# Bucketed attention and two dense layers on one core: preparing head pairs earlier and taking the products with v later

## The chip, the cores and the metric

The kernel runs on one core of a Trainium2 chip. Five engines matter here: TensorE (PE, with its weight loads PEld), VectorE (DVE), ScalarE (ACT), GpSimd (POOL) and SyncE (SP), which only issues transfers to the 16 DMA engines. The metric is device time in microseconds (us) for one execution; the lower the better.

## The reference

Two batches of eight heads, 768 positions, 64 numbers each. Queries and keys are hashed with six random projections; a query sees only the keys in its own bucket.

```
q_bits = (q @ proj > 0);  k_bits = (k @ proj > 0)        # six bits each
mask   = bucket(q_bits)[:, None] == bucket(k_bits)[None, :]
scores = where(mask, q @ k.T / sqrt(D), -1e9)
attn   = exp(scores - max(scores));  attn /= sum(attn) + 1e-9
x      = attn @ v                                        # (B, H, S, D) -> (B*S, 512)
h = x @ w_in1;  x = (h * sigmoid(1.702 * h)) @ w_out1    # 512 -> 2048 -> 512
h = x @ w_in2;  x = (h * sigmoid(h)) @ w_out2
```

The weights arrive as 64-bit floats and are turned into pairs of 32-bit tiles (high part, low part) on the chip.

## The kernel before

The attention is cut into 96 steps: 16 heads of six query chunks of 128 rows. Heads go in pairs, twelve steps to a pair, and the first 48 steps are the first batch. A step passes through these functions:

- `scores(j)`: four matmuls on PE into two PSUM banks (L417, L418); the second of each two adds the mask through the rows of bits in BQ and BK.
- `top(j)`: DVE takes the row minimum and writes the tile p (L425). `exps(j)`: ACT takes the exponential in place (L430).
- `p_high(j)`: ACT or DVE rounds p to 16 bits into one half of a tile hl (L439, L441). `p_low(j)`: POOL writes the rest into the other half (L445). One hl tile holds two steps.
- `p_turn(j)`: on every second step SP issues one DMA transpose of 128 x 3072 16-bit numbers, hl to pt (L451).
- `av(j)`: 18 pairs of weight load and matmul on PE, in three kinds (L463 to L465), multiply pt with the scaled v in VS.
- `norm(g)`: after the last step of a group DVE divides, PE turns the result (L491), ACT and DVE split it into XH and XL (L497, L498), the inputs of the dense layers.

Before a pair's steps, its preparation `ahead(pr, s)` is spread over steps s from -4 to 7: `natural` rounds and splits q and k as loaded, `turn` and `evict` transpose them through PE and ACT, `move` brings them into BQ (a transfer on SP) and BK (a copy on ACT) in the first batch, `bits` and `signs` make the hash bits, and `rows` issues four transfers on SP that put them into BQ and BK. `v_max`, `v_spread`, `v_scale` find the scale of v; `v_high` (ACT, L396) and `v_low` (DVE, L405) write the scaled v into VS. There are two VS tiles, so a pair writes over the one of two pairs before.

The loop emits the work of position i in an order written out by hand: scores of step i + 2, products with v of step i - LAG, and so on. A planner then sorts each engine's instructions by this order, moved up by the offsets in SOONER, and by its own picture of the time. Each engine runs its list in order. SP's list holds the transposes, the loads, the moves, the rows, the fetched weights (L139) and the spilled ones (L186).

From the end of the first batch's loop (SWITCH) the tiles of the pool att2 are given back, and the first layer on the first batch (`mlp`, L632 for the first product, L666 for the second, L637 for the first gate activation) is interleaved with the second batch's attention. After that the rest of both layers runs alone. MORE gives how many extra tiles of a kind the pool att2 holds during the first batch.

Of the kernel before, what the change touches and what calls it, by code (L numbers as in the profile page):

```python
# [10 lines left out]
F32R = mybir.dt.float32r  # L11
# [10 lines left out]
def tile_lsh_attention_two_mlps(  # L22
# [13 lines left out]
    V, A, G, T, SP = nc.vector, nc.scalar, nc.gpsimd, nc.tensor, nc.sync  # L36

    B, H, S, D = q.shape
    NB = proj.shape[1]
    NT, DM = out.shape  # L40
    DFF = w_in1.shape[1]
    P = 128
    NC = S // P
    HS = S // 2
    HC = NC // 2
    HEADS = B * H
    NPAIR = H // 2
    NDC = DM // P
# [3 lines left out]
    TB = HS  # L52
# [7 lines left out]
    QSCALE = -1.0 / math.sqrt(D)  # L60
    assert math.frexp(QSCALE)[0] == -0.5
    NBUF = 3
    LAG = 3
    TUL = 1
    MORE = {'aq': 1, 'ak': 1, 'p': 1, 'hl': 1, 'pt': 0, 'nk': 1, 'nq': 1, 'nv': 1}
    PTB = 2
    EARLY = 0
    WSTART = 38
# [10 lines left out]

    SOONER = ({'ahead': 100, 'move': 20, 'load_v': 400, 'evict': 200, 'p_high': 200, 'natural': 800, 'p_turn': 35, 'turn': 100, 'p_low': 75, 'top': 35, 'exps': 75, 'bits': 300, 'norm': 35, 'load': 50, 'signs': 20}, {'scores': 200, 'evict': 50, 'norm': 300, 'av': 400, 'natural': 200, 'gate': 50, 'p_turn': 20, 'load_v': 200, 'load': 20, 'sum': 150, 'move': 20, 'p_high': 150, 'rows': 100, 'p_low': 75, 'bits': 100, 'exps': 20}, {'gate': 300, 'sum': 10, 'weights': 50})  # L80
    RATE = (3.4, 2.85)
    SWITCH = HEADS // 2 * NC + LAG + 1
    RING = 3
    RING2 = 6

# [6 lines left out]
    xpool = ctx.enter_context(tc.tile_pool(name="x", bufs=1))  # L92
    wpool = ctx.enter_context(tc.tile_pool(name="w", bufs=RING))
    spill = ctx.enter_context(tc.tile_pool(name="spill", bufs=1, space=bass.MemoryType.DRAM))

    XH = [xpool.tile([P, NDC, TB], F32R, name=f"XH{i}") for i in range(NT // TB)]
    XL = [xpool.tile([P, NDC, TB], F32R, name=f"XL{i}") for i in range(NT // TB)]

# [151 lines left out]
    def attention(sp, s1, ps_m, ps_v, ahead_of, setup):  # L252
        nat, st = {}, {}
# [12 lines left out]
        N = len(steps)  # L266
# [141 lines left out]
        def scores(j):  # L408
            n, c = steps[j]
            aq, ak = st["q", n], st["k", n]  # L410
            bq, bk = BQ[place(n)], BK[place(n)]
            ps = ahead_of["pool"].tile([P, 2, 512], F32, tag="s", name="pss")
            lq = aq.rearrange("p a b -> p (a b)")[:, c * P:(c + 1) * P]
            bq = bq[:, c * P:(c + 1) * P]
            for half in range(2):
                o = ps[:, half, 0:HS]
                T.matmul(o, lhsT=lq, rhs=ak[:, half, :], start=True, stop=False)  # L417
                T.matmul(o, lhsT=bq, rhs=bk[:, half * HS:(half + 1) * HS], start=False, stop=True)  # L418
            st["S", j] = ps[:, :, 0:HS]


# [32 lines left out]
        def av(j):  # L454
            (n, c), g = steps[j], group[j]
            vs, s = st["v", n // 2]
            pt = st.pop(("pt", j))
            if j == g[0]:
                st["av", g] = v_bank("pav")
            o = st["av", g][:, c * (D + 1):(c + 1) * (D + 1)]  # L460
            for i in range(NC):
                hv, lv = vs[:, n % 2, i, 0:D + 1], vs[:, n % 2, i, D + 1:]
                T.matmul(o, lhsT=pt[:, i], rhs=hv, start=(i == 0), stop=False)  # L463
                T.matmul(o[:, 0:D], lhsT=pt[:, i], rhs=lv, start=False, stop=False)  # L464
                T.matmul(o, lhsT=pt[:, NC + i], rhs=hv, start=False, stop=(i == NC - 1))  # L465


        def norm(g):
# [32 lines left out]
        asked = set()  # L501
# [6 lines left out]
        def ahead(pr, s):  # L508
            a, b = 2 * pr, 2 * pr + 1

            two = bool(ahead_of["more"]) and b + 2 < HEADS // 2 + 2
            loads = {
                1: [(load, a + 2, "k"), (load, b + 2, "k")],
                3: [(load, a + 2, "q"), (load, b + 2, "q")],
                4: [(load_v, pr + 1)],
            } if two else {
                -3: [(load, b, "k")],
                -1: [(load, b, "q")],
                1: [(load, a + 2, "k")],
                3: [(load, a + 2, "q")],  # L520
                8: [(load_v, pr + 1)],
            }
            return [(f, *x) for f, *x in {
                -4: [(natural, a, "k")],
                -3: [(turn, a, "k", 0)],
                -2: [(evict, a, "k", 0), (turn, a, "k", 1), (natural, a, "q")],
                -1: [(evict, a, "k", 1), (turn, a, "q", 0), (v_max, pr)],
                0: [(evict, a, "q", 0), (turn, a, "q", 1), (natural, b, "k"), (move, a, "k")],
                1: [(evict, a, "q", 1), (turn, b, "k", 0)],
                2: [(turn, b, "k", 1), (v_spread, pr), (natural, b, "q"), (move, a, "q")],  # L530
                3: [(evict, b, "k", 0), (evict, b, "k", 1), (turn, b, "q", 0), (v_scale, pr)],
                4: [(evict, b, "q", 0), (turn, b, "q", 1), (v_high, pr, 0), (move, b, "k")],
                5: [(evict, b, "q", 1), (bits, pr, 0), (v_low, pr, 0)],
                6: [(signs, pr, 0), (bits, pr, 1), (v_high, pr, 1), (move, b, "q")],
                7: [(signs, pr, 1), (rows, pr), (v_low, pr, 1)],
            }.get(s, []) + [l for l in loads.get(s, []) if l[1:] not in asked and not asked.add(l[1:])]]

        def run(fs):
            for f, *a in fs:
# [40 lines left out]
            run(ahead(1, s))  # L580


        for lead, first, last in ((2, 0, N // 2), (1, N // 2, N)):
            def at(f, j):
                if first <= j < last:
                    with sooner(f.__name__):
                        f(j)

            for i in range(first - lead, last + LAG + 1):
                if lead == 2:  # L590
                    at(scores, i + 2)
                at(av, i - LAG)
                at(top, i + lead - 1)
                m = i - LAG
                if first <= m < last and m == group[m][-1]:
                    with sooner("norm"):
                        norm(group[m])
                m = i - 2 * (2 - lead)
                if first <= m < last:
                    pr, s = divmod(m, 2 * NC)  # L600
                    with sooner("ahead"):
                        if pr + 1 < HEADS // 2:
                            run(ahead(pr + 1, s))
                        if s >= 2 * NC - 4 and pr + 2 < HEADS // 2:
                            run(ahead(pr + 2, s - 2 * NC))
                at(exps, i)
                at(p_high, i)
                at(p_low, i)
                at(p_turn, i - TUL)
                yield i  # L610
                if lead == 1:
                    at(scores, i + 1)
# [87 lines left out]
    work = [None]  # L700
# [20 lines left out]
    with ExitStack() as es:  # L721
# [10 lines left out]
        for i in attention(sp, s1, ps_m, ps_v, ahead_of, lambda: attention_setup(sp, s1, am, ps_m)):  # L732
# [3 lines left out]
            if gen is None and i >= WSTART and i % WEVERY == 0 and W.done < 4:  # L736
                W.step()
            if gen is None and i == SWITCH - 1:
                ps_s.close()
                ps_v.pop()  # L740
                stage[0] = 1
                ahead_of["lead"] = 1
                ahead_of["more"] = {}
                mb = es.enter_context(tc.tile_pool(name="mlpb", bufs=2))
                ahead_of["pool"] = es.enter_context(tc.tile_pool(name="ps_s1", bufs=1, space=PSUM))
                ps_h = es.enter_context(tc.tile_pool(name="ps_h", bufs=2, space=PSUM))
                work[0] = es.enter_context(tc.tile_pool(name="ps_w", bufs=1, space=PSUM))
                gen = mlp(0, [0, 1], [[f, f + 1] for f in range(0, NF, 2)], W, mb, ps_h, True, first1)
# [48 lines left out]
```

## Time and profile before

| | us |
|---|---|
| median of three runs | 806.92 (805.03 to 807.02) |
| the profiled execution's own time | 809.91 |
| its span, first to last instruction | 807.9 |

The kernel's time is that of the whole execution. The profile's times count from the first instruction; its rows are those of one execution. A row of a timeline has start, duration, engine (a q behind it marks the engine's queue of issues), line, operation and tiles; what stands in brackets is the engine's idle time before it and who ended it. Rows of the same instruction that follow each other without a gap are merged, with their count behind an x.

### The profile page before, as it was taken

The numbers are of one execution on the slowest core, as the hardware profiler recorded it, in microseconds if no ns is written. First come the engines' busy times: TensorE is split into PE (matmuls) and PEld (weight loads), VectorE is DVE, ScalarE is ACT, GpSimd is POOL, SyncE is SP. The second block draws the span as 40 slices with busy tenths as digits, with TensorE's granted clock in tenths as the row PEclk, the third lists the DMA queues.
The fourth block names the chain that finished last, engine by engine and source line by source line (L and its number), as shares of the span: only waits on it lengthen the run. The fifth ranks groups of instructions, "written<-read, shape, count | busy, mean of one in ns | idle before, by whom it ended". The sixth has DMA issues, their size and how long they took to land.

```text
span 807.9 us, 14034 instructions
## 1 busy us (share of the span) xinstructions
PE 740.4 (92%) x5384; PEld 682.6 (84%) x5384; DVE 507.3 (63%) x932; ACT 422.4 (52%) x721; POOL 430.4 (53%) x345
## 2 busy tenths in 40 slices
PE   6786777678889999899999999979999999999998
PEld 5676666668878898899899999978998899989996
DVE  8987688967689798887332244999545744322222
ACT  6776576586778586676444134445545333311220
POOL 5675567877659666766633133567535334422220
PEclk9898888799999999999999999999999999999999
DMA  5999999999999998885597040333211300000112
GB/s 160 206 191 186 185 204 208 211 247 249 272 225 252 255 227 239 220 188 106 149 387 246 2 157 1 130 108 101 80 52 53 105 1 2 0 1 1 40 40 78
DMA packets 196270, 116.40 MB, mean 144 GB/s; under 512 B 153318, under 2 KB 175846, under 8 KB 196204
## 3 DMA queue, kind: packets, MB, share of 16 engines
q1 hardware_dynamic: 196044, 115.52, 57.5%
q8 instruction: 42, 0.69, 0.3%
q14 instruction: 24, 0.20, 0.1%
q10 hardware_dynamic: 160, 0.00, 0.0%
HBM read 56.63 MB, written 16.78 MB: 91 GB/s over the span
## 4 chain that ended last, share of the span: by engine, by line
PE 66%; DMA 13%; DVE 10%; issue 4%; ACT 3%; POOL 2%; SPq 0%; ACTq 0%; DVEq 0%; POOLq 0%
PE pso L666 29%; PE psh L632 28%; DMA pt<-hl 9%; PE pss L417 2%; PE psbit L345 2%; POOL hl L445 2%; DMA raw<-in_moe_w_in_dram 2%; DVE p L425 2%; PE pss L418 2%; DVE f L176 1%; ACT p L430 1%; PE pav L463 1%; PE pav L464 1%; PE pav L465 1%; DVE f L175 1%
## 5 line engine op out<-in xcount | busy, mean ns | idle before, releaser
L643 POOL TENSOR_TENSOR gl<-g,gh 128x384 fp32r<-128x384 f32 x128 | 136.0, 1064 | 195.7 <-ACT gh L642 183.6
L445 POOL TENSOR_TENSOR hl<-p,hl 128x768 f16<-128x768 f32 x96 | 162.6, 1700 | 71.9 <-ACT hl L441 37.4
L632 PE MATMUL psh<-XH,wih 128*128 128x384 f32 x512 | 174.2, 340 | 1.5 <-DVE part L675 1.0
L632 PE MATMUL psh<-XL,wih 128*128 128x384 f32 x512 | 172.9, 338 | 1.8 <-DVE XL L498 1.8
L632 PE MATMUL psh<-XH,wil 128*128 128x384 f32 x512 | 173.2, 338 | 0.0
L675 DVE SCALAR_TENSOR_TENSOR part<-pso,part 128x384 f32<-128x384 f32 (+1 forms) x124 | 72.6, 591 | 88.8 <-PE pso L666 88.6
L641 DVE TENSOR_TENSOR g<-g,psh 128x384 f32<-128x384 f32 x96 | 52.8, 551 | 117.5 <-ACT g L640 117.5
L430 ACT ACTIVATE p<-p,lo 128x768 f32<-128x768 f32 x96 | 89.7, 936 | 52.7 <-DVE p L425 52.2
L642 ACT CAST gh<-g 128x384 fp32r<-128x384 f32 x128 | 65.5, 513 | 78.7 <-DVE g L641 69.1
L425 DVE TENSOR_SCALAR_CACHE_REDUCE p<-pss 128x768 f32<-128x768 f32 x96 | 90.8, 948 | 15.3 <-PE pss L418 13.3
L632 PEld LDWEIGHTS psh<-XH,wih 128*128 128x128 f32 x512 | 97.5, 190 | 3.1 <-ACT XH L677 1.0
L632 PEld LDWEIGHTS psh<-XL,wih 128*128 128x128 f32 x512 | 97.6, 191 | 2.8 <-DVE XL L498 2.2
L632 PEld LDWEIGHTS psh<-XH,wil 128*128 128x128 f32 x512 | 97.3, 190 | 0.2 <-POOL wil L181 0.2
L640 ACT ACTIVATE g<-psh 128x384 f32<-128x384 f32 x96 | 46.8, 489 | 96.1 <-PE psh L632 95.2
L463 PE MATMUL pav<-VS,pt 128*128 128x65 f16 x576 | 64.4, 198 | 33.9 <-DMA pt<-hl 32.1
L666 PE MATMUL pso<-gh,woh 128*128 128x384 f32 x256 | 87.3, 347 | 6.5 <-ACT gh L642 4.3
L463 PEld LDWEIGHTS <-pt 128*128 128x128 f16 x576 | 54.6, 99 | 44.1 <-DMA pt<-hl 38.9
L666 PE MATMUL pso<-gh,wol 128*128 128x384 f32 x256 | 86.2, 337 | 0.0
L666 PE MATMUL pso<-gl,woh 128*128 128x384 f32 x256 | 86.1, 336 | 0.0
L417 PE MATMUL pss<-ak,aq 128*128 128x384 f32 x192 | 76.0, 397 | 10.8 <-DVE p L425 10.5
L666 PE MATMUL pso<-woh,gh 128*128 128x512 f32 x192 | 74.8, 390 | 0.2 <-ACT gh L642 0.2
L666 PE MATMUL pso<-wol,gh 128*128 128x512 f32 x192 | 75.0, 391 | 0.0
(119 smaller groups left out, 1572.0 us busy)
## 6 DMA issues: line engine op xcount, KB each, us to landing
raw<-in_moe_w_in_dram SPq DMA_DIRECT2D x32, 512.0 KB
raw<-in_moe_w_out_dram SPq DMA_DIRECT2D x32, 512.0 KB
spih<-wih SPq DMA_DIRECT2D x13, 256.0 KB
spil<-wil SPq DMA_DIRECT2D x13, 256.0 KB
spoh<-woh SPq DMA_DIRECT2D x13, 256.0 KB
spol<-wol SPq DMA_DIRECT2D x13, 256.0 KB
wih<-spih SPq DMA_DIRECT2D x13, 256.0 KB
wil<-spil SPq DMA_DIRECT2D x13, 256.0 KB
```

Source lines behind the costliest of these rows:

```text
L417: T.matmul(o, lhsT=lq, rhs=ak[:, half, :], start=True, stop=False)
L425: V.tensor_scalar(p, st.pop(("S", j)), LOW, None, op0=ALU.min, op1=ALU.min, accum_out=lo)
L430: A.activation(p, p, AF.Exp, bias=lo, scale=-1.0)
L445: G.tensor_tensor(out=hl[:, 1], in0=st.pop(("p", j))[0], in1=hl[:, 0], op=ALU.subtract)
L463: T.matmul(o, lhsT=pt[:, i], rhs=hv, start=(i == 0), stop=False)
L632: T.matmul(h, lhsT=a[:, c], rhs=x[t][:, c], start=(n == 0), stop=(n == 3 * NDC - 1))
L640: A.activation(g, h, AF.Sigmoid, scale=beta)
L641: V.tensor_tensor(out=g, in0=g, in1=h, op=ALU.mult)
L642: A.copy(gh[:, f], g)
L643: G.tensor_tensor(out=gl[:, f], in0=g, in1=gh[:, f].bitcast(F32), op=ALU.subtract)
L666: T.matmul(y, lhsT=a, rhs=x, start=(n == 0), stop=(n == 3 * nf - 1))
L675: V.scalar_tensor_tensor(out=acc, in0=y, scalar=scale, in1=acc, op0=ALU.mult, op1=ALU.add)
```

## The change

LAG becomes a pair, 7 in the first batch and 3 in the second, and in the first batch each `av(j)` is held on PE behind the last scores matmul of step j + 9 where that one exists. The preparation of pairs 2, 3 and 4 (counted from 0) runs three positions sooner, except for `v_high`, `v_low` and the loads. MORE gives one more extra tile for p (now four in all) and hl (four), and two for pt (four where there were two). XH2, XH3, XL2 and XL3 move into a pool that is opened at the switch, which comes four positions later in the written order.

```diff
-    LAG = 3
+    LAGS = (7, 3)
     TUL = 1
-    MORE = {'aq': 1, 'ak': 1, 'p': 1, 'hl': 1, 'pt': 0, 'nk': 1, 'nq': 1, 'nv': 1}
+    SOON = 3
+    MORE = {'aq': 1, 'ak': 1, 'p': 2, 'hl': 2, 'pt': 2, 'nk': 1, 'nq': 1, 'nv': 1}
...
-    SWITCH = HEADS // 2 * NC + LAG + 1
+    SWITCH = HEADS // 2 * NC + LAGS[0] + 1
...
-    XH = [xpool.tile([P, NDC, TB], F32R, name=f"XH{i}") for i in range(NT // TB)]
-    XL = [xpool.tile([P, NDC, TB], F32R, name=f"XL{i}") for i in range(NT // TB)]
+    XH, XL = [], []
+
+    def x_tiles(pool):
+        for i in range(len(XH), len(XH) + NT // TB // 2):
+            XH.append(pool.tile([P, NDC, TB], F32R, name=f"XH{i}"))
+            XL.append(pool.tile([P, NDC, TB], F32R, name=f"XL{i}"))
+
+    x_tiles(xpool)
...
-                T.matmul(o, lhsT=bq, rhs=bk[:, half * HS:(half + 1) * HS], start=False, stop=True)
+                st["did", j] = T.matmul(o, lhsT=bq, rhs=bk[:, half * HS:(half + 1) * HS], start=False, stop=True).ins
...
-            for i in range(NC):
-                hv, lv = vs[:, n % 2, i, 0:D + 1], vs[:, n % 2, i, D + 1:]
-                T.matmul(o, lhsT=pt[:, i], rhs=hv, start=(i == 0), stop=False)
-                T.matmul(o[:, 0:D], lhsT=pt[:, i], rhs=lv, start=False, stop=False)
-                T.matmul(o, lhsT=pt[:, NC + i], rhs=hv, start=False, stop=(i == NC - 1))
+
+            first = st.get(("did", j + 9)) if j < N // 2 else None
+            with tc.issue_after(first) if first is not None else nullcontext():
+                for i in range(NC):
+                    hv, lv = vs[:, n % 2, i, 0:D + 1], vs[:, n % 2, i, D + 1:]
+                    T.matmul(o, lhsT=pt[:, i], rhs=hv, start=(i == 0), stop=False)
+                    T.matmul(o[:, 0:D], lhsT=pt[:, i], rhs=lv, start=False, stop=False)
+                    T.matmul(o, lhsT=pt[:, NC + i], rhs=hv, start=False, stop=(i == NC - 1))
...
+            k = s + (SOON if 2 <= pr <= HEADS // 4 else 0)
+            work = {
...
-                4: [(evict, b, "q", 0), (turn, b, "q", 1), (v_high, pr, 0), (move, b, "k")],
-                5: [(evict, b, "q", 1), (bits, pr, 0), (v_low, pr, 0)],
-                6: [(signs, pr, 0), (bits, pr, 1), (v_high, pr, 1), (move, b, "q")],
-                7: [(signs, pr, 1), (rows, pr), (v_low, pr, 1)],
-            }.get(s, []) + [l for l in loads.get(s, []) if l[1:] not in asked and not asked.add(l[1:])]]
+                4: [(evict, b, "q", 0), (turn, b, "q", 1), (move, b, "k")],
+                5: [(evict, b, "q", 1), (bits, pr, 0)],
+                6: [(signs, pr, 0), (bits, pr, 1), (move, b, "q")],
+                7: [(signs, pr, 1), (rows, pr)],
+            }.get(k, [])
+            work += {
+                4: [(v_high, pr, 0)],
+                5: [(v_low, pr, 0)],
+                6: [(v_high, pr, 1)],
+                7: [(v_low, pr, 1)],
+            }.get(s, [])
+            return work + [l for l in loads.get(s, []) if l[1:] not in asked and not asked.add(l[1:])]
...
-        for lead, first, last in ((2, 0, N // 2), (1, N // 2, N)):
+        for lead, first, last, LAG in ((2, 0, N // 2, LAGS[0]), (1, N // 2, N, LAGS[1])):
...
-                        if s >= 2 * NC - 4 and pr + 2 < HEADS // 2:
+                        if s >= 2 * NC - 4 - SOON and pr + 2 < HEADS // 2:
                             run(ahead(pr + 2, s - 2 * NC))
...
                 ps_v.pop()
+                x_tiles(ctx.enter_context(tc.tile_pool(name="x2", bufs=1, side="right")))
```

## Rows read from the trace of the kernel before

**Rows 1.** The page: busy time of each engine with its share of the span and number of instructions, and the span in 40 equal slices, the busy share of each in tenths, for PE and for the DMA engines.

```profile
PE 740.4 (92%) x5384; PEld 682.6 (84%) x5384; DVE 507.3 (63%) x932; ACT 422.4 (52%) x721; POOL 430.4 (53%) x345
...
PE   6786777678889999899999999979999999999998
...
DMA  5999999999999998885597040333211300000112
```

**Rows 2.** The windows: busy time of each engine in four stretches (start:end and length in us), then the granted clock of PE, the DMA engines' share and GB/s.

```profile
20.00:167.00 147.00, 111.74 (x1243) 96.50 (x1244) 120.71 (x225) 98.38 (x144) 99.78 (x64) 0.85 0.99 200
167.00:200.00 33.00, 26.59 (x300) 23.79 (x299) 23.98 (x48) 26.09 (x45) 24.01 (x20) 1.00 1.11 245
200.00:400.00 200.00, 188.93 (x1659) 176.59 (x1658) 157.27 (x310) 138.97 (x228) 138.54 (x109) 0.99 0.89 213
400.00:808.00 408.00, 399.44 (x2109) 375.27 (x2107) 188.43 (x292) 146.24 (x285) 156.56 (x137) 1.00 0.24 81
```

**Rows 3.** The waits from 20 to 167 us: who waited for whom, us in total, times, longest.

```profile
PE pav L463 <- DMA pt<-hl: 20.0, 10, 4.0
```

**Rows 4.** The timeline of SP: the first and the last of the 75 issues between 20.2 and 167 us, two transposes that follow each other, and the transpose of the first batch's last two steps (162.06).

```profile
20.22 3.72 SPq L451 DMA_TRANSPOSE pt<-hl  x1
...
107.68 4.89 SPq L451 DMA_TRANSPOSE pt<-hl  x1
112.75 3.65 SPq L451 DMA_TRANSPOSE pt<-hl  x1
...
162.06 4.82 SPq L451 DMA_TRANSPOSE pt<-hl  x1
166.94 0.57 SPq L186 DMA_DIRECT2D spil<-wil  x1
```

**Rows 5.** The timeline of POOL: the end of the low halves for the steps behind those transposes (the first row is the first of the three merged in the second).

```profile
105.28 1.65 POOL L445 TENSOR_TENSOR hl<-p,hl 128x768 f16<-128x768 f32 x1
105.28 4.88 POOL L445 TENSOR_TENSOR hl<-p,hl 128x768 f16<-128x768 f32 x3
...
153.26 3.75 POOL L445 TENSOR_TENSOR hl<-p,hl 128x768 f16<-128x768 f32 x2
```

**Rows 6.** The view of SP's own waits from 20 to 167 us: what its next issue waited for, us in total, times, longest.

```profile
SPq L451 <- POOL hl L445: 47.9, 18, 5.0
...
SPq L451 <- PE pav L465: 1.4, 1, 1.4
```

**Rows 7.** The timeline of SP around the places where it stood still, and two pairs of transposes with what was issued ahead of them (L360 the rows, L281 the loads of q and k, L329 the moves).

```profile
69.12 0.74 SPq L360 DMA_DIRECT2D BK<-mk  x1
70.32 0.77 SPq L360 DMA_DIRECT2D BQ<-mk  x1
...
75.64 0.84 SPq L281 DMA_DIRECT2D nq<-in_q_dram  x2
76.58 0.53 SPq L329 DMA_DIRECT2D BQ<-aq  x1
77.22 9.91 SPq L451 DMA_TRANSPOSE pt<-hl  x2
...
88.51 0.37 SPq L281 DMA_DIRECT2D nq<-in_q_dram  x1
89.90 0.85 SPq L360 DMA_DIRECT2D BK<-mk  x1
90.86 7.57 SPq L451 DMA_TRANSPOSE pt<-hl  x2
...
120.92 0.58 SPq L281 DMA_DIRECT2D nk<-in_k_dram  x1
122.37 0.33 SPq L281 DMA_DIRECT2D nq<-in_q_dram  x1
123.05 0.84 SPq L360 DMA_DIRECT2D BK<-mk  x1
...
140.34 0.74 SPq L360 DMA_DIRECT2D BQ<-mk  x1
141.19 0.52 SPq L329 DMA_DIRECT2D BK<-ak  x1
143.12 3.68 SPq L451 DMA_TRANSPOSE pt<-hl  x1
```

**Rows 8.** The instructions of line 451 from 20 to 167 us: duration in ns (least, median, most), first and last start in us.

```profile
L451 SPq DMA_TRANSPOSE pt<-hl x24: 3617/4200/5539, 20.2 to 162.1; - x24
```

**Rows 9.** The timelines of ACT and PE at the switch: the first gate activation, and the first and the last group of the products with v of the first batch's last two steps.

```profile
168.93 0.87 ACT L637 ACTIVATE g<-psh 128x384 f32<-128x384 f32 x2 [0.69 <-DMA pt<-hl]
...
168.88 0.20 PE L463 MATMUL pav<-VS,pt 128*128 128x65 f16 x1 [1.44 <-DMA pt<-hl]
...
169.90 0.19 PE L463 MATMUL pav<-VS,pt 128*128 128x65 f16 x1
```

**Rows 10.** The waits from 167 to 200 us.

```profile
PE pav L463 <- DMA pt<-hl: 4.6, 3, 1.8
```

**Rows 11.** The timelines of PE and ACT around the end of the first pair: the first product of its last two steps, the last scores matmul of step 20, and ACT writing the second half of the third pair's scaled v.

```profile
58.56 0.20 PE L463 MATMUL pav<-VS,pt 128*128 128x65 f16 x1 [0.94 <-DMA pt<-hl]
...
62.94 0.34 PE L418 MATMUL pss<-BK,BQ 128*128 128x384 f32 x1
...
61.22 0.60 ACT L396 ACTIVATE VS<-nv,sv 128x384 f16<-128x384 f32 x1
```

More of the change, by code (lines that the diff above doesn't have):

```diff
@@ L522, in ahead @@
             }
-            return [(f, *x) for f, *x in {
+            k = s + (SOON if 2 <= pr <= HEADS // 4 else 0)
+            work = {
                 -4: [(natural, a, "k")],
```

## Prediction

> **What bounds the kernel now.** I began with the page. The span is 807.9 us, and PE, DVE, ACT and POOL are busy for 92, 63, 52 and 53% of it, but the slices show two regimes [rows 1]. In the first eight slices PE stands at 6 to 8 tenths while the DMA engines stand at 9; from slice 16 on PE is at 9 and DMA falls away. The windows cut this into stages [rows 2]. From 20 to 167 us (the first batch's attention) PE is busy 111.7 of 147 us, no other engine more than 120.7, the granted clock is 0.85 of full (part of the stage at 1.2 GHz, the rest at 2.4) and the DMA share 0.99. From 200 us to the end PE is busy 188.9 + 399.4 of 608 us, 97%: there the time is the sum of matmuls, which the change leaves alone. So the question is when the first stage lets go.
>
> The view of waits for that stage offers a suspect: PE stands 20.0 us for transposed tiles (pt from hl) [rows 3]. That is the wait which nine steps of distance would remove. But who makes pt late? SP issues every transpose, in order. Its timeline is nearly gapless. Between 20.22 and 166.94 us there are 75 issues, 24 of them transposes, whose durations sum to 135.4 of 146.7 us; the first and the last of them and two that follow each other are in [rows 4]. A hop between two issues is 0.1 to 0.2 us (112.57 to 112.75), some 8 us over 75.
>
> The second test is whether SP waits for its input. POOL finished two hl pairs at 106.93 (105.28 + 1.65) and 110.16 (105.28 + 4.88) [rows 5]; their transposes were issued at 107.68 and 112.75 [rows 4]: 0.7 and 2.6 us after the input was ready. The last pair of the batch was ready at 157.01 [rows 5] and issued at 162.06 [rows 4], 5 us late. The queue is the late one. The view of SP's own waits says otherwise, 47.9 us for POOL's hl [rows 6]. The timeline shows no such holes, and I read that entry as signals of later hl tiles that arrive while a transpose is already being issued. I keep the doubt as a rival.
>
> **The change, part by part.** The later products, issue_after, the larger tile counts and the move of XH2, XH3, XL2, XL3 into a pool opened at the switch add no instruction to any queue. They change when something may start.
>
> *Products with v, nine steps behind the scores, with four pt, hl and p tiles where there were two, three and three.* This removes PE's 20.0 us of waits. It shortens the kernel only if SP thereby gets its transposes out sooner. The one place in the stretch shown where SP stood for a pt tile is the 1.41 us between 141.71 and 143.12 [rows 7], which the view of waits books as 1.4 us on PE's pav, once [rows 6]. The extra hl and p tiles let DVE, ACT and POOL run further ahead; that costs and brings nothing while SP's backlog covers it, 0.7 to 5 us at the three places above, and where the cover is gone POOL's own 1.65 us for one step of hl [rows 5] is the price of a late step.
>
> *Pairs three to five prepared three steps sooner.* Per pair this moves four casts and splits, eight turns and evictions, the k copies on ACT, the bits and signs, and on SP two moves of q and four row transfers. On SP those six pass one or two transposes: 4 x 0.80 + 2 x 0.53 = 4.3 us that a transpose then stands behind, given back when the old place is reached. For the whole stage the sum on SP is unchanged. Even pair five's rows were out at 140.34 + 0.74 [rows 7], before the batch's last transpose, so no work crosses that mark. What it can remove is SP standing for preparation that isn't ready. The holes are 69.86 to 70.32, 88.88 to 89.90, 121.50 to 122.37 and 122.70 to 123.05 [rows 7]: 0.46 + 1.02 + 0.87 + 0.35 = 2.70 us, each ahead of a row transfer or a load that needs a piece of the preparation. On POOL and DVE the moved splits go ahead of hl work, again under SP's backlog.
>
> *Sum of the holes.* 1.41 + 2.70 = 4.11 us; less five ordinary hops of 0.1, 3.6 us. Bounds are 0 (the holes reappear elsewhere) and 3.6; I take 3.6, since each hole ends with a piece that now comes three steps sooner or with a tile of which there are now two more.
>
> *What a transpose costs to issue.* The 24 take 3.62 to 5.54 us, median 4.20 [rows 8]. Two in a row behind row transfers take 7.57 us together; two behind loads of q and a move take 9.91 [rows 7]. So the extra follows the plain transfers just ahead, and they remain. If all of it went, 24 x (4.20 - 3.62) = 13.9 us would go. Bounds 0 and 13.9; I take 0, by the two pairs of rows. The page "DMA: Bandwidth & Descriptors", section "Latency and other measured facts", in the Trainium skill gives a DMA transpose an effective 261 GB/s. By that a tile of 128 x 3072 halves needs an estimated 3.0 us of the DMA engines. By it the engines would have time left and the extra need not be a backlog of data, so the sum could reach the full 13.9 us. No transpose here goes out faster than 3.62 us, and the trace decides.
>
> *The switch.* The first gate activation waited until 168.93 for the last transpose's landing, and the last products began at 168.88 [rows 9]. With two pt tiles in the pool that the second layer's buffers replace, the gate may wait until those are read: until 169.90 + 0.19 for the last group [rows 9], so +1.2 us at most. I take 0 and keep 1.2. Earlier splits free the load buffers sooner, so a load may slip ahead of the last transpose: 0.55 us of issue and up to about 0.5 of extra each.
>
> *What is late next.* With SP 3.6 us ahead, the last transpose would go at about 158.5, still after its input at 157.0 [rows 5], so POOL doesn't take over. From 167 to 200 us PE waits 4.6 us on pt again [rows 10], behind the same SP queue, so those waits shift along. After 200 us PE is 97% busy and passes a shift on one for one.
>
> The profiled execution took 809.91 us around its 807.9 span; the runs have a median of 806.92. I apply the difference to the median: 806.9 - 3.6 = 803.3, **803 us**.
>
> **Rivals.**
> *Larger gain.* The 47.9 us in SP's waits are real, or the extra spreads out: with deeper tiles SP never waits in an issue. For it speaks [rows 6]; against it, that long and short issues sort by what stands ahead [rows 7]. Half of 13.9 gives 803.3 - 7 = 796; all of it 789.
> *No change.* The DMA engines are full (share 0.99 [rows 2]) and the holes only let them catch up, or the switch eats the gain: -3.6 + 1.2 + two loads at 1.05 = -0.3, 806.6. For it: the DMA share. Against: it also reads 1.11 from 167 to 200, so 0.99 isn't a ceiling.
> *Slower.* The second half of each pair's scaled v is written into a tile that the last product two pairs back still reads. Before, that product ran from 58.56 us and ACT wrote at 61.22 [rows 11]. Now it must follow scores which then ended at 62.94 + 0.34 = 63.3 [rows 11], so with 1.2 us of its own it ends near 64.5, and ACT's and DVE's queues, with exps and casts behind, stand 3.3 us. SP's backlog covers most of it, but at 107.68 it was only 0.7. Three pairs at 3.3 - 0.7 make 7.8: 803.3 + 7.8 = 811. It decides where SP's backlog falls under 3.3 us. Against: four p tiles let the scores run earlier.
>
> **How the numbers follow.** About 0.3% (2.4 us) is what a measurement of this kernel tells from no change, so below 804.5 counts as faster. Chances: forecast 0.40 (its own range 801 to 804.5), larger gain 0.17, no change 0.24, slower 0.19. Faster is 0.40 + 0.17 = 0.57, same 0.24, slower 0.19. The range leaves out the deeper half of the larger gain and the far end of the slower case: 793 to 811.
>
> **What the profile after would show.** Right: PE's wait on pt before 167 us falls from 20 to under 5; SP's issues still fill over 95% of the stage, with the five holes gone; the transposes' median stays near 4.2; the batch's last transpose goes out near 158 instead of 162.06; PE's busy time after 200 us is as before. Larger gain: the median falls toward 3.7. No change: PE's wait is gone and the last transpose still goes out near 162. Slower: ACT waits on pav ahead of the scaled v, and transposes are issued the moment hl ends. I would be wrong in kind if SP had idle time in the stage and the end still moved.

## The result and the profile after

The changed kernel takes 816.52 us (median of four executions, 812.20 to 818.13) where the kernel before has 805.97 on the same occasion: a ratio of 1.0128, 95% interval 1.0080 to 1.0177. The forecast was 803, faster. The change costs some 10 us, and the result lies above the end of the range (811).

The profiled execution of the changed kernel shows only a part of this. It took 812.20 us around a span of 810.4, beside 809.91 around 807.9 before: 2.3 us more. A later profile of the same program took 812.97, while its other executions took 815.6 to 821.2. So what the traces place is the smaller part of the loss, and the rest is looked for with timed kernels below.

The page after (as [rows 1], with PE's granted clock), and the windows (as [rows 2]):

```profile
PE   7688686687799999899999999989999999999998
...
PEclk9789997899999999999999999999999999999999
DMA  5999999999999999986795040432211300000112
```

```profile
20.00:167.00 147.00, 109.33 (x1246) 92.51 (x1247) 120.16 (x228) 101.96 (x152) 100.89 (x64) 0.88 0.98 197
167.00:200.00 33.00, 26.34 (x263) 23.77 (x262) 22.60 (x43) 22.98 (x40) 22.52 (x19) 0.95 1.08 261
200.00:400.00 200.00, 187.13 (x1687) 175.86 (x1687) 155.34 (x310) 138.80 (x227) 139.19 (x109) 1.00 0.94 220
400.00:808.00 408.00, 402.18 (x2111) 378.06 (x2109) 188.59 (x292) 146.30 (x285) 157.54 (x137) 1.00 0.23 77
```

PE's busy time in the first stage falls from 111.7 to 109.3 us for nearly the same number of matmuls, with the clock at 0.88 where it was 0.85; DVE, ACT and POOL are busy for within 4% of what they were. The loss begins in the second window: from 167 to 200 us PE runs 263 matmuls where it ran 300, and the clock, 1.00 before, is 0.95. The count overstates it, since matmuls differ in length: in the trace of before, at full clock and where the next follows at once, a product with v takes 29 to 33 ns and one that writes psh 173. By such times, an estimate of the work done, the 263 are 23.7 us and the 300 are 24.7. The change thus loses here the lead of 1.0 us that it had won by 167 us.

The waits from 20 to 167 us (as [rows 3]):

```profile
ACT p L439 <- DVE p L434: 20.1, 14, 3.2
...
PE pss L426 <- DVE p L434: 14.4, 14, 1.9
...
PE pav L475 <- DMA pt<-hl: 12.0, 7, 3.7
```

The wait on pt shrank from 20.0 to 12.0 us, and the wait for DVE's row minimum (pss from p) now stands above it.

SP's timeline around the end of the first batch (as [rows 4, 7]); start, duration, engine, line, operation and tiles:

```profile
145.53 4.11 SPq L460 DMA_TRANSPOSE pt<-hl  x1
151.41 0.33 SPq L195 DMA_DIRECT2D spih<-wih  x1
...
152.96 5.83 SPq L460 DMA_TRANSPOSE pt<-hl  x1
...
160.49 5.16 SPq L460 DMA_TRANSPOSE pt<-hl  x1
...
167.33 5.71 SPq L460 DMA_TRANSPOSE pt<-hl  x1
...
175.96 5.41 SPq L460 DMA_TRANSPOSE pt<-hl  x1
...
183.01 0.58 SPq L290 DMA_DIRECT2D nq<-in_q_dram  x1
183.65 0.48 SPq L301 DMA_DIRECT2D nv<-in_v_dram  x1
...
185.46 8.19 SPq L460 DMA_TRANSPOSE pt<-hl  x1
...
199.43 3.82 SPq L460 DMA_TRANSPOSE pt<-hl  x1
```

POOL's rows for hl (as [rows 5]):

```profile
141.26 3.26 POOL L454 TENSOR_TENSOR hl<-p,hl 128x768 f16<-128x768 f32 x2 [0.82 <-DVE hl L448]
```

The last pair of hl tiles was ready at 144.52 (141.26 + 3.26), and its transpose went out at 160.49: 16.0 us late where before it was 5.0 late [rows 4, 5]. The inputs came 12.5 us sooner, the transpose 1.6. So the queue on SP is indeed what bounds the stage. There is also a new hole in it, from 149.64 (145.53 + 4.11) to 151.41, ahead of the spill of a weight tile.

After the switch the second batch goes out later than before. Its third and fourth transposes are issued at 185.46 and 199.43, before at 181.64 and 191.40 (SP's timeline before):

```profile
181.64 4.31 SPq L451 DMA_TRANSPOSE pt<-hl  x1
...
191.40 3.69 SPq L451 DMA_TRANSPOSE pt<-hl  x1
```

The rows of DVE and PE there after the change, with the idle time and its releaser in brackets:

```profile
188.31 0.93 DVE L314 CAST sq<-nq 128x384 fp32r<-128x384 f32 x1 [2.19 <-DMA nq<-in_q_dram]
...
191.08 0.95 DVE L386 TENSOR_REDUCE am<-nv 128x2 f32<-128x768 f32 x1 [0.77 <-DMA nv<-in_v_dram]
...
193.28 0.95 DVE L434 TENSOR_SCALAR_CACHE_REDUCE p<-pss 128x768 f32<-128x768 f32 x1
```

```profile
194.29 0.44 PE L426 MATMUL pss<-ak,aq 128*128 128x384 f32 x1 [4.05 <-DVE p L434]
...
206.58 0.20 PE L475 MATMUL pav<-VS,pt 128*128 128x65 f16 x1 [2.78 <-DMA pt<-hl]
```

The 13th load of q is issued on SP at 183.01, behind the transposes of 167.33 and 175.96; before, it was issued at 122.37 [rows 7]. DVE stands 2.19 us for it, then 0.77 for v, and only then takes the row minimum at 193.28. PE stands 4.05 us for that and 2.78 us for a pt tile later on. Before, nothing in this stretch kept PE that long: its longest wait for p is 0.5 us from 167 to 240 us:

```profile
PE pss L417 <- DVE p L425: 0.8, 2, 0.5
```

The other traces of the change's order, of kernels told of below, have the pattern: the wait for q's load is 2.4, 3.8 and 4.1 us, and PE's wait for p there 3.0, 3.1 and 4.1 us (e10_change_again, e16_change_aligned, e18_change_to_400).

This wait isn't the whole loss, and PE's idle time alone doesn't show it. From 167 us to the first product of the first layer on the second batch (at 399.15 before, at 399.44 after) PE stands 17.5 us before, and 18.8, 16.0 and 13.9 us in after, e10_change_again and e16_change_aligned. Two of these three spend more of that time at the lower of PE's two clock levels (1.2 of 2.4 GHz, a granted clock of 0.5): 3.4 us before, and 3.4, 9.0 and 10.6 us. By the estimate of work used above, the four traces with the change's order fall behind the four with the order of before (before, e14_pool_only, e15_pool_aligned, e17_before_to_400) at three places: 13.8 to 15.2 us of work against 16.8 to 17.8 from 180 to 200 us, 14.2 to 16.4 against 16.9 to 18.2 from 320 to 340, and 17.7 to 18.0 against 19.4 to 19.6 from 360 to 380. From 260 to 280 us they do more, 17.9 to 18.2 against 14.7 to 17.4.

### The profile page after: what moved, and what is told of

The parts are those of the page before. It is cut to its first block, busy times and chain, and to the rows that moved or that the text cites. A ratio compares the mean times of both kernels' runs of the same rounds, so it can differ in the third digit from the quotient of the medians.

```text
span 810.4 us, 14020 instructions
## 1 busy us (share of the span) xinstructions
PE 739.2 (91%) x5384; PEld 681.1 (84%) x5384; DVE 504.4 (62%) x932; ACT 422.0 (52%) x721; POOL 430.9 (53%) x345
## 4 chain that ended last, share of the span: by engine, by line
PE 61%; DMA 15%; DVE 13%; issue 5%; ACT 3%; POOL 2%; SPq 1%; DVEq 0%; POOLq 0%; ACTq 0%
PE psh L654 26%; PE pso L688 25%; DMA pt<-hl 11%; DVE p L434 2%; PE pss L426 2%; PE pss L427 2%; DVE f L185 2%; DMA nv<-in_v_dram 1%; DVE f L187 1%; PE pav L475 1%; PE psbit L354 1%; PE pav L476 1%; PE pav L477 1%; DVE f L183 1%; DMA nk<-in_k_dram 1%
## 5 line engine op out<-in xcount | busy, mean ns | idle before, releaser
L454 POOL TENSOR_TENSOR hl<-p,hl 128x768 f16<-128x768 f32 x96 | 162.3, 1700 | 64.3 <-ACT hl L450 34.5
L426 PE MATMUL pss<-ak,aq 128*128 128x384 f32 x192 | 74.1, 388 | 19.1 <-DVE p L434 18.8
L475 PE MATMUL pav<-VS,pt 128*128 128x65 f16 x576 | 67.6, 200 | 26.0 <-DMA pt<-hl 25.3
```

The costliest lines, as they stand in the source:

```text
L454: G.tensor_tensor(out=hl[:, 1], in0=st.pop(("p", j))[0], in1=hl[:, 0], op=ALU.subtract)
```

## The experiments

**Parts of the change.** Four kernels leave parts of it out. Against the kernel after:

```diff
# e2_soon_only: XH2.. stay in the first pool; tile counts of before; no hold
-    LAGS = (7, 3)
+    LAGS = (3, 3)
-    MORE = {'aq': 1, 'ak': 1, 'p': 2, 'hl': 2, 'pt': 2, 'nk': 1, 'nq': 1, 'nv': 1}
+    MORE = {'aq': 1, 'ak': 1, 'p': 1, 'hl': 1, 'pt': 0, 'nk': 1, 'nq': 1, 'nv': 1}
# e3_no_soon
-    SOON = 3
+    SOON = 0
# e4_no_hold
-            first = st.get(("did", j + 9)) if j < N // 2 else None
+            first = None
# e5_tiles_only
-    LAGS = (7, 3)
-    SOON = 3
+    LAGS = (3, 3)
+    SOON = 0
```

> Only the earlier preparation of pairs three to five; distance 3, the tile counts and all four XH and XL as before. Preparation theory (the rows and moves that now stand sooner in SP's list and the turns in PE's cost the time): 813 to 818 us, as the whole change. Lag theory (the products taken later let the other engines run ahead of SP, and the switch pays): 805 to 808. Tiles theory (only the new places and counts of the tiles matter): 805 to 808. The last transpose of the first batch would be issued near 165 us by the first, near 162 by the others.

Measured: 819.2 us, ratio 1.0157 (1.0131 to 1.0184), above every range. The batch's last transpose went out at 162.09, not near 165, and its input was ready only at 161.41 (159.75 + 1.66), where before it was ready at 157.01 [rows 5]. The earlier preparation alone brings hl later and uses up SP's backlog:

```profile
159.75 1.66 POOL L455 TENSOR_TENSOR hl<-p,hl 128x768 f16<-128x768 f32 x1
```

```profile
162.09 5.18 SPq L461 DMA_TRANSPOSE pt<-hl  x1
```

> The whole change without the earlier preparation. Preparation theory: 804 to 808 us. Lag theory: 813 to 818. Tiles theory: 813 to 818. By the prediction's own sum (holes on SP's list vanish) it would be 804 to 806 at best, since only the 1.4 us hole at the pt tile goes.

Measured: 814.42, ratio 1.0105 (1.0072 to 1.0138). The preparation theory fails. The batch's last transpose goes out at 157.57, 4.5 us sooner than before.

> The whole change, but the products with v are not held behind the scores of step j + 9 on PE; the written order still has them seven steps behind. If the hold is what costs (v's second half, the v tiles and the pt tiles come free too late, PE does the products in bunches): 804 to 808 us. Preparation, lag and tiles theories: 813 to 818.

Measured: 817.37, ratio 1.0152 (1.0127 to 1.0176), in the range of the other theories.

> Only the tile counts (pt four, hl four, p four) and the second pool for XH2, XH3, XL2, XL3; distance 3, nothing prepared sooner. Tiles theory: 813 to 818 us. Preparation and lag theories: 804 to 808. By the prediction's sum: the hole of 1.4 us at the pt tile goes, 804 to 806.

Measured: 810.56, ratio 1.0057 (1.0032 to 1.0082), between the two ranges. The last transpose goes out at 156.69, 5.4 us sooner than before.

No part is free, and the parts don't add up: the early preparation alone costs 1.57%, the rest without it 1.05%, both together 1.28%. The hold is not the culprit, since without it the kernel is no faster. That speaks against a single wait brought in by one edit, and for something that any edit disturbs. Two things qualify this. All but e2_soon_only hold the move of XH2, XH3, XL2 and XL3, which costs some 2.1 us by itself, as is measured further down, so that about 0.3% is left of e5_tiles_only's loss. And the load of q that comes late in the change comes late in all four (178.5 to 185.0 us), but DVE stands for it 0.5 us at most, so a loss of this size doesn't need that wait.

The windows of e2_soon_only:

```profile
190.00:200.00 10.00, 8.38 (x80) 7.50 (x78) 7.55 (x16) 6.49 (x11) 8.75 (x7) 1.00 1.10 248
200.00:210.00 10.00, 6.74 (x47) 5.32 (x48) 6.95 (x13) 5.02 (x7) 6.58 (x5) 0.55 0.91 212
210.00:220.00 10.00, 7.93 (x69) 7.76 (x69) 4.82 (x8) 5.57 (x12) 2.28 (x2) 0.84 1.00 241
220.00:230.00 10.00, 10.00 (x69) 9.74 (x68) 7.90 (x16) 8.74 (x15) 7.26 (x5) 0.93 0.85 222
```

```profile
201.41 0.69 PE L427 MATMUL pss<-ak,aq 128*128 128x384 f32 x1 [3.03 <-DVE p L435]
...
204.91 0.24 PE L476 MATMUL pav<-VS,pt 128*128 128x65 f16 x1 [1.86 <-DVE u L184]
```

PE stood 3.03 us for DVE and soon after 1.86 us again; from 200 to 210 us the granted clock was 0.55 where it had been 1.00. It was at the lower level from 201.0 to 211.3 us, and once more from 218.1 to 221.5, after PE had stood 2.07 us for pt until 216.68.

**Is any new order worse?** The planner makes the order of every engine's list from the offsets in SOONER. Two kernels change one of these in the kernel before, by a tenth, and nothing else; in their traces 1,491 and 1,245 of PE's 5,384 matmuls stand at another place of its list than before (2,165 in the change), up to the end of the second batch's attention.

```diff
-    SOONER = ({... 'turn': 100, ...
+    SOONER = ({... 'turn': 110, ...        # e6_turn_110; 90 in e7_turn_90
```

> The kernel before with one planner offset of the first batch changed (turn 110 instead of 100): no step moved by hand, no tile added, yet the planner orders the first batch anew, about as many places of PE's list as the change with earlier preparation alone. Replanning theory (any new order of the first batch leaves SP at the switch in another state, PE then stands in pieces of 2 to 6 us in the second batch, the granted clock falls behind each, and the loss follows from that): 809 to 819 us, with 15 to 30 us at half clock after 165 us. Specific theory (only the parts of the change cost): 804 to 809.

> The same with turn 90. Replanning theory: 809 to 819 us. Specific theory: 804 to 809.

Measured: 814.02, ratio 1.0088 (1.0054 to 1.0122), and 821.62, ratio 1.0174 (1.0140 to 1.0208). A nudge with no meaning of its own costs 7 and 14 us, as much as the change. Of the thirteen orders of the whole kernel that were timed in this study, that of before is the fastest.

The clock's part in this theory isn't borne out. After 165 us the trace of e6_turn_110 has 9.0 us at the lower clock level, where before has 8.4 and 15 to 30 were expected; that of e7_turn_90 has 15.0, the low end of what was expected. In both the 13th load of q goes out as before (121.3 and 123.4 us), and PE's longest wait from 167 to 400 us is 2.3 and 2.5 us. So these runs show what a new order costs, and not by which wait.

**Can the second batch be mended?** It waits for pt as the first did. Five kernels put its products with v later, in the kernel before and in the kernel after, by position alone or held behind later scores as the change does in the first batch.

```diff
-    LAG = 3
+    LAGS = (3, 5)        # e8_later_second, e11_hold_second; (3, 4) in e12; (7, 5) in e9 and e13
...
+            first = st.get(("did", j + 5)) if j >= N // 2 else None     # e11; j + 4 in e12
+            first = st.get(("did", j + (9 if j < N // 2 else 5)))       # e13
...
```

> The kernel before with the products with v five steps behind in the second batch (three before), the first batch's order untouched. If PE's waits on transposed tiles after the switch and the clock that falls behind them set the loss in the second batch: 797 to 803 us, with PE's waits on pt between 167 and 400 us down from about 11 us to under 4. If they are only the place where another limit (SP, DVE) shows: 804 to 810.

Measured: 814.47, ratio 1.0091 (1.0057 to 1.0125), above both ranges. PE's wait on pt from 167 to 400 us is 9.3 us, before 12.1, so the later place by itself hardly removes it.

> The whole change with the products with v five steps behind in the second batch. If the loss of the change lies in PE's waits on transposed tiles after the switch: 802 to 808 us against 816.5 for the change. If it lies in the first batch, or in other waits after the switch: 813 to 818.

Measured: 815.80, ratio 1.0104 (1.0069 to 1.0138), in the second range.

> The kernel before; in the second batch the products with v are written five steps behind and held on PE behind the last scores of step j + 5. First batch as before. Clock theory: PE's waits on pt between 160 and 400 us fall from 12.3 to under 5 us and the half clock stays under 4 us, 799 to 804 us. Replanning theory alone (any new order of the second batch is worse than the one of before, whatever it is meant to do): 810 to 816 us. A rival: the held products give the pt tiles (two) back late, SP's transposes wait for them, and the attention ends later: over 812, with transpose 48 issued after 390 us (386 before).

Measured: 811.09, ratio 1.0043 (1.0022 to 1.0065), as the replanning theory has it. The half clock is 6.8 us, not under 4. The rival of the pt tiles fails: the last transpose goes out at 375.6 us.

> The same with four steps in place of five. Clock theory: waits on pt under 7 us, 800 to 806 us. Replanning theory alone: 810 to 816. The rival of the two pt tiles: between the kernel before and the run with five.

Measured: 814.80, ratio 1.0083 (1.0054 to 1.0111), again as by replanning; the wait on pt is 10.4 us, not under 7.

> The whole change with the same hold of five steps in the second batch. Clock theory: 801 to 807 us, since the first batch ends no later than before. Replanning theory alone: 811 to 820.

Measured: 818.72, ratio 1.0138 (1.0113 to 1.0164), in the range of replanning.

The largest waits of PE from 160 to 400 us, before (one) and in e11_hold_second (three):

```profile
PE pav L463 <- DMA pt<-hl: 12.3, 11, 2.3
```

```profile
PE pso L668 <- DVE g L640: 3.5, 2, 3.3
PE pss L417 <- DVE p L425: 3.0, 4, 1.9
PE pav L465 <- DMA pt<-hl: 2.9, 4, 1.2
```

In e11_hold_second the hold does what it should: the wait for pt falls from 12.3 to 2.9 us, and the last product with v ends at 384.1 us, before at 393.8. Yet the time is 0.4% longer. The attention ends 10 us sooner, and the layer that runs beside it has by then done 24 products with the first and 45 with the second weights fewer than before at the attention's end; they run afterwards. A wait removed from one of two interleaved streams isn't time gained.

**The same kernel once more.**

> The changed kernel again, for a second trace of it: its first trace was of an execution that was 4 us faster than its median. Clock theory (after the switch PE stands in pieces longer than 2 us, the granted clock halves behind them, and it is this that makes the loss): 814 to 818 us, and a trace near the median shows over 10 us at half clock between 160 and 400 us, against 3.4 before and 6.8 in the first trace. If the clock is no part of it, half clock stays near 7 us and the extra time stands as idle time of PE.

Measured: 817.64, ratio 1.0117 (1.0087 to 1.0148), so the result repeats. The trace is again of a fast execution (812.97). It has 13.7 us at the lower level between 160 and 400 us, 6.9 of them from 162.3 to 169.2, around the switch. That is the sign which the clock theory asked for, but not in an execution near the median, so it doesn't settle what the slower ones lose.

**The place of four tiles.** In the layers that run alone, from 550 to 800 us, all kernels have the same order, and still the change's trace is behind there. The windows of the products that write psh, from 550 to 800 us, in before, e14_pool_only, after and e16_change_aligned (busy us and count of PE first):

```profile
550.00:800.00 250.00, 127.92 (x720) 125.65 (x720) 34.03 (x62) 29.76 (x61) 1.00 0.12 40
```

```profile
550.00:800.00 250.00, 128.81 (x720) 126.31 (x718) 33.54 (x61) 29.71 (x61) 1.00 0.12 40
```

```profile
550.00:800.00 250.00, 129.03 (x720) 126.71 (x720) 34.12 (x62) 29.76 (x61) 1.00 0.11 39
```

```profile
550.00:800.00 250.00, 127.76 (x720) 125.48 (x720) 34.06 (x62) 29.70 (x61) 1.00 0.12 40
```

The same 720 products take 127.9 us before and 129.0 after. Their instructions are the same, but XH2, XH3, XL2 and XL3 lie elsewhere: in the new pool XH2 begins at address 204768, which is 32 past a multiple of 64; before, at 28800, a multiple of 64. The second and the fourth row are of kernels made to test this. e14_pool_only takes from the change nothing but the move of these tiles, with every engine's list as before; e15_pool_aligned adds a pad of 32 bytes, and e16_change_aligned adds the pad to the whole change.

```diff
+                ctx.enter_context(tc.tile_pool(name="pad", bufs=1, side="right")).tile([P, 8], F32, name="pad")
                 x_tiles(ctx.enter_context(tc.tile_pool(name="x2", bufs=1, side="right")))
```

> The kernel before, with XH2, XH3, XL2 and XL3 alone moved to the second pool on the right (XH2 then begins at address 204768, which is 32 past a multiple of 64; before at 28800, a multiple of 64); every engine has the instructions of before in the order of before. Place theory (the layers' products that read a moved tile take about 3 ns longer each, some 768 of them, so 2.3 us): 808 to 809 us beside a kernel before of 806.3, +0.3%; in 550 to 800 us the psh products of blocks 2 and 3 start 176 ns apart where those of blocks 0 and 1 start 173 apart. Rival (the spacing in the traces is no price, the loss of the change is all order): within 0.1% of before, though the spacing may show.

Measured: 808.55, ratio 1.0027 (1.0006 to 1.0047).

> As e14_pool_only, with a pad of 32 bytes ahead of the second pool, so that XH2 begins at 204736, a multiple of 64; the order is that of before. If the offset of 32 bytes is what costs: the time of before (806.3), blocks 2 and 3 at 173 to 174 ns. If the distance or the place on the right is what costs: as e14_pool_only, 808 to 809, blocks 2 and 3 at 176 ns. Rival (the place costs nothing): e14_pool_only, this one and before are all alike.

Measured: 806.49, ratio 0.9990 (0.9970 to 1.0010).

> The kernel after, with the same pad of 32 bytes and nothing else; its order is that of after. If the offset costs 2.3 us: 814 to 815 us where after has 816.5 to 817.6, a ratio of 1.009 to 1.010 to before. If the place or nothing of it costs: 816.5 to 817.6, a ratio of 1.012 to 1.013. In either case the second batch's loss stays, so that it is over 1.006.

Measured: 812.44, ratio 1.0068 (1.0044 to 1.0092).

The place costs, and by its offset: at a multiple of 64 the tiles may lie on the right for nothing. Half of the 720 products read them, so one takes (128.81 - 127.92) / 360 = 2.5 ns longer in e14_pool_only and (129.03 - 127.92) / 360 = 3.1 ns in the change. In the two layers 768 products read them: 1.9 to 2.4 us, where the timed difference of e14_pool_only and e15_pool_aligned is 2.1 by the medians (by the ratios 3.0, give or take 2.3). In the change the pad gave back 4 to 5 us by the medians, more than expected; the interval (1.0117 against 1.0068, each known to about 0.3%) doesn't exclude 2.4.

The traces of all seventeen whole kernels agree. From the first product of the first layer on the second batch to the last instruction they take 408.4 to 409.4 us in the nine whose tiles begin at a multiple of 64 (e15_pool_aligned and e16_change_aligned among them), and 410.9 to 411.7 us in the eight where they begin 32 bytes past one. The order makes no difference there, so in these traces what it costs is paid ahead of these layers.

**Where the other 6 us lie.** Two kernels stop after the second batch's attention: the first layer on the second batch and the second layer are left out, and XH is written out instead.

```diff
-    stage[0] = 2
...
+    for t in range(NT // TB):
+        SP.dma_start(out=out[t * TB:(t + 1) * TB].rearrange("(p r) e -> p (r e)", p=P), in_=XH[t].rearrange("p c f -> p (c f)").bitcast(F32))
```

> The kernel before without what follows the second batch's attention: the first layer on the second batch and the whole second layer are left out, and the four tiles XH are written out in their place. Every engine has before's list up to there; only the last transposes on SP and the writing stand otherwise. About 400 us for the part that before's trace ends at 394 (last product with v) to 403, and some 5 for the writing: 405 us, a ratio of 0.50. It is the base of e18_change_to_400.

Measured: 405.65 (403.85 to 407.25); its ratio to the whole kernel before is 0.5011 (0.4994 to 0.5029).

> e16_change_aligned cut in the same way. Theory (what the change loses is lost in the second batch, in the order that the planner made anew, also where no trace has it): 5 to 6 us more than e17_before_to_400, as e16_change_aligned takes 5.95 more than e15_pool_aligned. Rival (it is lost in the layers that run alone, whose order is the same, by a lower clock or by contention): within 1.5 us of e17_before_to_400, or sooner.

Measured: 407.77 (406.47 to 411.27); ratio 0.5032 (0.5019 to 0.5045).

Up to the end of the attention the change costs 2.1 us by the medians; by the ratios 0.0021 x 809 = 1.7, give or take 1.8. That lies between the 5 to 6 us of the one theory and the rival's "within 1.5", and is hardly clear of noise. The traces of both, in two windows:

```profile
167.00:240.00 73.00, 66.02 (x620) 60.08 (x619) 55.14 (x108) 55.00 (x93) 49.22 (x38) 0.95 1.05 251
200.00:400.00 200.00, 189.56 (x1694) 177.90 (x1694) 159.78 (x314) 141.04 (x232) 141.33 (x110) 0.99 0.91 226
```

```profile
167.00:240.00 73.00, 63.01 (x541) 58.09 (x540) 49.27 (x97) 48.32 (x84) 42.27 (x35) 0.89 1.04 251
200.00:400.00 200.00, 189.39 (x1703) 178.86 (x1700) 155.16 (x312) 138.63 (x226) 137.44 (x107) 0.97 0.92 219
```

In this pair the loss stands where the first trace had it: from 167 to 240 us 541 matmuls instead of 620 (by the estimate above 53.3 us of work instead of 59.0), at a clock of 0.89 instead of 0.95. But e18_change_to_400's trace is of its slowest execution (411.27), so that the pair is 6.2 us apart where the medians are 2.1.

The whole kernel loses some 6 us with the same lists (6.3 by the ratios of e16_change_aligned and e15_pool_aligned, give or take 2.5). The 4 us between the two results stay open, and by the two intervals they may be much less. The mean granted clock of the timed executions is lower with the change (0.960 in e16_change_aligned, 0.968 in before beside it), so that PE spends (0.968 - 0.960) x 811 / 0.5 = 13 us more at the lower of its two levels. In the two cut kernels it is 0.927 and 0.939, so some 10 us of these lie ahead of the attention's end. A part of the rest may be paid behind it, though no trace shows the layers there to take longer with the change's order.

## Why the prediction was wrong

Point by point:

- **SP bounds the first stage: right for the kernel before and the change.** In all whole kernels run here the batch's last transpose goes out between 156.7 and 164.2 us, whether products with v, tiles or preparation come sooner or later; in after its input was ready 16.0 us ahead of it. Only in e2_soon_only is the input nearly as late as SP (0.7 us). Removing PE's waits on pt gave no time, as said. They fell only to 12.0, not below 5: held nine steps back, PE still meets the backlog of the transposes.
- **The holes, 3.6 us: mis-sized.** The five are gone, but new ones stand elsewhere, the largest of 1.77 us at 149.64. All holes over 0.3 us from 20 to 167 us sum to 4.1 us after and 4.7 before. The 4.7 hold a sixth, of 0.56 us at 160.20, that the prediction left out; its 75 issues are 79 in the trace, while their sum of 135.4 us is right. The last transpose went out 1.6 us sooner, not 3.6. Over the traces of whole kernels it is less: 160.5, 160.9 and 162.0 with the change's order, and 161.4, 162.1 and 162.5 with that of before. "Bounds are 0 (the holes reappear elsewhere) and 3.6" held; the value taken was the far end.
- **Issue time of a transpose, 0: right.** The 24 take 3.65 to 5.83 us, median 4.09 (before 4.20). The larger gain falls with that. By the 261 GB/s of the page "DMA: Bandwidth & Descriptors", section "Latency and other measured facts", in the Trainium skill, a figure for a transpose with a non-contiguous middle dimension, the data of one need an estimated 3.0 us. The shortest issue of one in any run here is 3.56 us (e2_soon_only).
- **The switch, 0 with 1.2 at most: too small.** The first gate activation starts at 170.85 instead of 168.93 [rows 9], 1.9 us later although the last transpose was sooner. It now waits last for a product with v, which is the wait for which the prediction kept its 1.2 us. This is more than the holes gave.

```profile
170.85 0.87 ACT L659 ACTIVATE g<-psh 128x384 f32<-128x384 f32 x2 [0.34 <-PE pav L477]
```

- **"After 200 us PE is 97% busy and passes a shift on one for one": the step that failed.** It took the second batch's lists as given and the shift as the only thing that reaches them. The last transpose goes out 4.5 us sooner than before in e3_no_soon and 5.4 us sooner in e5_tiles_only, and these kernels are 1.05% and 0.57% slower (some 0.3% of each is the place of the four tiles): the shift isn't passed on. The lists are made anew up to the second batch's end: q's load stood 60 us later on SP, DVE waited for it ahead of the row minimum, PE for DVE. "those waits shift along" [rows 10] took only the wait for pt into account, and not that another instruction would be first in a queue. The runs with a changed offset show that such an order costs 7 and 14 us without any change in what is computed, which was no case of the forecast.
- **"the move of XH2, XH3, XL2, XL3 into a pool opened at the switch add no instruction to any queue": true, and mis-sized.** It costs 0 instructions and 2.1 us (e14_pool_only against e15_pool_aligned), over half of the forecast gain.
- **The slower rival: the right sign by another mechanism.** ACT waited 1.0 us for a product with v ahead of the scaled v, once, against the 8 us of the rival; and without the hold (e4_no_hold) the kernel is as slow.

What is shown: the cost of the offset, the changed loads and waits in the trace, that new orders cost as much as the change, and that the traces have this cost ahead of the layers that run alone. What is not shown is which waits make up the loss. The wait for p behind q's load (4.05 us in after) stands in every trace of the change's order, but e2_soon_only, e3_no_soon, e6_turn_110 and e7_turn_90 lose 7 to 14 us without the wait for q's load, and no run has the change with that one load back in its place. That part of the cause stays open.

## What to carry to other kernels

Where a planner orders the lists, an edit's price has two parts: what it does by itself, and that the tuned order is lost; nudge an offset that means nothing, time it, and take that spread as the noise that a forecast must contain. When a tile moves, look at its address as well as at the instructions that read it. And in a stage where two streams share the busy engine, a shorter wait in one counts only if the sum of both becomes shorter.

## What the hardware showed

A float32 product of 128 x 384 takes 2.5 to 3.1 ns longer when the tile that it reads begins 32 bytes past a multiple of 64 (720 products, half of them moved: 128.8 and 129.0 us instead of 127.9), and none of it is left with a pad of 32 bytes (127.8). One offset, 32 bytes, was tried.

A wait in a stage that PE fills can be paid again in what follows it. In e2_soon_only PE stood 3.03 us until 201.41 and 1.86 us until 204.91, and its granted clock was at the lower level from 201.0 to 211.3 us: 0.55 in the window from 200 to 210. In after it stood 4.05 us until 194.29, and the lower level lasted from 194.8 to 198.2. It isn't always so: in e6_turn_110 PE stood 2.28 us until 201.37, and the clock is 1.00 from 196 to 230 us.
